# One token loop for q and k, DRAM-source transposes, and a do-projection moved into the attention loop: a linear-attention and MQA gradient kernel on one core

## The chip, the cores and the metric

The kernel runs on one core of one Trainium2 chip. The metric is the time of one execution on the device in microseconds (us); lower is better.

Terms: PE is TensorE and PEld its weight load, DVE is VectorE, ACT is ScalarE, POOL is GpSimd, SP is SyncE. "SPq" and "ACTq" are these engines' sequencers at work on issuing DMAs. The profile names a DMA transpose DMA_TRANSPOSE and an ordinary copy DMA_DIRECT2D; the trace holds a record of every packet that the DMA engines moved, with its size and duration.

## The reference, cut to what matters

Two attention blocks stand side by side, their outputs are concatenated, and all gradients are wanted (nine outputs in all). A is linear attention (16 heads of 28), B is softmax attention with one shared key and value head. S is 2048 tokens, D is 448, everything is bf16.

```python
def _A_ref(x, wqkv, wo):
    qkv = (x @ wqkv).reshape(B, S, 3, H, Dh) ...          # q, k, v
    phi = lambda t: jnp.where(t > 0, t + 1, jnp.exp(t)) + 1e-6
    pq, pk = phi(q), phi(k)
    kv = jnp.einsum("bhsd,bhse->bhde", pk, v);  z = jnp.einsum("bhsd->bhd", pk)
    o = einsum(pq, kv) / (einsum(pq, z)[..., None] + 1e-6)
    return o.reshape(B, S, D) @ wo
def _B_ref(x, wq, wk, wv, wo):
    # q has 16 heads, k and v one head; softmax(q k^T / sqrt(Dh)) v, then @ wo
...
_out, _vjp = jax.vjp(_f, ...);  _grads = _vjp(grad_out)    # grad_out is [1, 2048, 896]: A's half, B's half
```

448 = 3 x 128 + 64. The matmuls here contract over at most 128 partitions at a time (128*128 in the trace), so each operand with 448 rows is kept as three full chunks and one of 64 rows.

## The kernel before

Phase A computes A forward and backward; `phase_B_pre` prepares B; a loop of 540 units does B's attention forward and backward; a tail makes the last projections. Operands that must have the feature dimension on the partitions are transposed by DMA out of SBUF, from tiles that are padded to 512 columns:

```python
def dma_T(dst, src, t0, n):                      # SBUF -> SBUF, 4 token tiles a call
    nc.sync.dma_start_transpose(dst[:, t0:t0 + n, :, :].rearrange("p t c k -> p (t c) k"),
                                src[:, t0:t0 + n, :].rearrange("p t d -> p (t d)"))
...
load_nat(ga, go2[:, 0:D], nc.sync)               # grad_out, A's half
...
nc.gpsimd.memset(t[:, :, D:512], 0.0)            # for t in (pk, pq, wq_n, ga): the padding
...
for q4 in range(4):
    dma_T(gaT, ga, 4 * q4, 4)
```

q is projected after k's loop, in four groups, with GpSimd at work on every token tile:

```python
def phi(ps, dst, eng):
    E = awk.tile([P, D], F32, name="phiE")
    nc.scalar.activation(out=E[:], in_=ps[:, :], func=ACT.Exp)
    eng.tensor_scalar(out=E[:], in0=E[:], scalar1=1.0, scalar2=1e-6, op0=ALU.min, op1=ALU.add)   # POOL for q
    nc.vector.scalar_tensor_tensor(out=dst, in0=ps[:, :], scalar=0.0, in1=E[:], op0=ALU.max, op1=ALU.add)
...
def den(q4):                                     # divides by the denominators
    ...
        nc.gpsimd.tensor_tensor(out=wd, in0=wd, in1=rb, op=ALU.mult)
        nc.vector.tensor_tensor(out=pv, in0=pv, in1=rb, op=ALU.mult)
    dma_T(pqpT, pq, 4 * q4, 4)
```

Three names recur. `st1` is the first matmul of A's backward loop over tokens (`KOT` with `gaT`). `out1` is the loop that writes the gradient of A's x, from `pkT`, `gqT` and `gkT`. The do-projection (`do_nat`) multiplies B's half of grad_out by wo and stands at the end of `phase_B_pre`:

```python
for st in range(NS):                             # 16 token tiles
    ps = gen([P, 512])
    for c in range(4):
        mm(ps[:, :], gbT[:, st, c, :], woTp[:, c, :], start=(c == 0), stop=(c == 3))
    nc.any.tensor_copy(out=do_nat[:, st, :], in_=ps[:, :])
```

Of the kernel before, what the change touches and what calls it, by code (L numbers as in the profile page):

```python
# [14 lines left out]
H = 16  # L15
# [9 lines left out]
def kernel(  # L25
# [50 lines left out]
    make_identity(nc, identF[:])  # L76
# [26 lines left out]

    def chunks_of(i):
        lo, hi = HR[i]
        return [k for k in range(4) if k * P < hi and k * P + DC_ROWS[k] > lo]
# [4 lines left out]
    def phase_A(pa, cA, awk, psA):  # L111
# [15 lines left out]
        xaT, tT, gaT, pqpT = v4(R2), v4(tTf), v4(gaB), v4(ppB)  # L127
        gkn = wq_n

        qs = [nc.sync, nc.scalar]  # L130
        for i in range(8):
            if i == 2:
                load_w(w3, A_wqkv, D, 2 * D, nc.scalar)
            qs[i % 2].dma_start(xa[:, 2 * i:2 * i + 2, 0:D],
                                Ax2[i * 256:(i + 1) * 256, :].rearrange("(t p) d -> p t d", p=P))
# [5 lines left out]
        nc.gpsimd.memset(xa[:, :, D:512], 0.0)  # L141
        nc.gpsimd.memset(xa[:, :, D:D + 16], 1.0)
        nc.gpsimd.memset(w3[64:128, 3, :], 0.0)
        nc.gpsimd.memset(w3[0:64, 3, 3 * D:1408], 0.0)
        nc.gpsimd.memset(w3[:, 0:3, 3 * D:1408], 0.0)
        for t in (pk, pq, wq_n, ga):
            nc.gpsimd.memset(t[:, :, D:512], 0.0)
# [26 lines left out]
        K1T = [ppB[:, 4 * i:4 * i + 4, :] for i in range(2)]  # L174
# [7 lines left out]
        for t in (kv_blk, kvT_blk, dkv_blk, KO, KOT, zrow, *ddT):  # L182
            nc.gpsimd.memset(t[:], 0.0)
        for i in range(2):
            nc.gpsimd.memset(K1T[i], 0.0)

# [15 lines left out]
        def phi(ps, dst, eng):  # L202
            E = awk.tile([P, D], F32, name="phiE")
            nc.scalar.activation(out=E[:], in_=ps[:, :], func=ACT.Exp)  # L204
            eng.tensor_scalar(out=E[:], in0=E[:], scalar1=1.0, scalar2=1e-6, op0=ALU.min, op1=ALU.add)  # L205
            nc.vector.scalar_tensor_tensor(out=dst, in0=ps[:, :], scalar=0.0, in1=E[:], op0=ALU.max, op1=ALU.add)

# [10 lines left out]

        k1acc = accs()
        xT(0)  # L220
        xT(1)
        for st in range(NS):
            if st + 2 < NS:
                xT(st + 2)
            phi(proj(st, D), pk[:, st, 0:D], nc.vector)
            if st >= 2:
                accmm(k1acc, xa, pk, st - 2)
        accmm(k1acc, xa, pk, NS - 2)
        accmm(k1acc, xa, pk, NS - 1)
        nc.vector.tensor_tensor(out=zrow[64:80, :], in0=k1acc[3][64:80, :], in1=mrow[64:80, :], op=ALU.mult)  # L230
        hilo(K1T, k1acc)
        for i in range(2):
            nc.sync.dma_start_transpose(K1[i][:].rearrange("p c h k -> p (c h) k"), flat(K1T[i]))
        for q4 in range(4):
            dma_T(gaT, ga, 4 * q4, 4)
# [24 lines left out]
        def qproj(q4):  # L260
            for st in range(4 * q4, 4 * q4 + 4):
                phi(proj(st, 0), pq[:, st, 0:D], nc.gpsimd)
            dma_T(tT, pq, 4 * q4, 4)

        def den(q4):
# [8 lines left out]
            for s in range(4):  # L274
                st = 4 * q4 + s
                rb = rden[:, st, :].unsqueeze(2).to_broadcast([P, H, DH])
                wd = wq_n[:, st, 0:D].rearrange("p (h e) -> p h e", e=DH)
                pv = pq[:, st, 0:D].rearrange("p (h e) -> p h e", e=DH)
                nc.vector.tensor_scalar(out=wq_n[:, st, 0:D], in0=pq[:, st, 0:D], scalar1=-1e-6, scalar2=1.0,
                                        op0=ALU.add, op1=ALU.min)  # L280
                nc.gpsimd.tensor_tensor(out=wd, in0=wd, in1=rb, op=ALU.mult)
                nc.vector.tensor_tensor(out=pv, in0=pv, in1=rb, op=ALU.mult)
            dma_T(pqpT, pq, 4 * q4, 4)

        qproj(0)
# [3 lines left out]
        qproj(1)  # L289
        blkprod(kv_blk, [lambda c, i: K1T[0][:, c, i * P:(i + 1) * P], lambda c, i: K1T[1][:, c, i * P:(i + 1) * P]],  # L290
                [lambda c: w3[:, c, 2 * D:3 * D]])
        den(0)
        qproj(2)
        prod_to(KOT, woA, kvT_blk, True)
        prod_to(KO, kvT_blk, woA, False)
        den(1)
        qproj(3)
        den(2)

        wvT = w_T(cA.tile([P, 4, D], BF16, name="wvT"), w3, 2 * D)  # L300
        woT = w_T(cA.tile([P, 4, D], BF16, name="woT"), woA, 0)
# [5 lines left out]
        def st1(st):  # L307
            ps = gen([P, D])
            for c in range(4):
                mm(ps[:, :], gaT[:, st, c, :], KOT[:, c, :], start=(c == 0), stop=(c == 3))  # L310
            tps[st] = ps
            pr = awk.tile([P, H, DH], F32, name="phiE")
# [4 lines left out]
        def st2(st):  # L317
            pt = gen([P, P], BF16)
            nc.tensor.transpose(pt[:, :], ga[:, st, 3 * P:512], identB[:, :], tile_position=(0, 0))
            nc.vector.tensor_copy(out=ddT[st % 3][64:80, :], in_=pt[64:80, :])  # L320
# [7 lines left out]
        def outA(st):  # L328
# [5 lines left out]
            nc.sync.dma_start(out0[st * P:(st + 1) * P, 0:D], ot[:])  # L334

        for i in range(NS + 2):
            if i == 2:
                den(3)
# [26 lines left out]
        def gw(gn, blk):  # L365
# [3 lines left out]
            for c in range(4):  # L369
                r = DC_ROWS[c]  # L370
                sb = awk.tile([P, 512], BF16, name="osb")[:, 0:D]
                nc.any.tensor_copy(out=sb[0:r, :], in_=al[c][0:r, :])
                nc.sync.dma_start(out_2[c * P:c * P + r, blk * D:(blk + 1) * D], sb[0:r, :])
# [4 lines left out]
        for st in range(NS):  # L378
# [3 lines left out]
            dph = awk.tile([P, 512], BF16, name="osb")[:, 0:D]  # L382
            nc.gpsimd.tensor_scalar(out=dph[:], in0=pk[:, st, 0:D], scalar1=-1e-6, scalar2=1.0, op0=ALU.add, op1=ALU.min)  # L383
            nc.vector.tensor_tensor(out=gkn[:, st, 0:D], in0=ps[:, :], in1=dph[:], op=ALU.mult)
        xb = pk
        nc.gpsimd.memset(xb[:, :, D:512], 0.0)
        load_nat(xb, Bx2, nc.sync)
        prod_to(VWT, dkvT_blk, wvT, False)
        blkprod(dkv_blk, [lambda c, i: GT[0][:, c, cs(i)], lambda c, i: GT[1][:, c, cs(i)]], [lambda c: woT[:, c, :]])
        gkT = gaT  # L390
# [24 lines left out]
        wst = dkv_blk  # L415
        load_w(wst, B_wq, 0, D, nc.sync)
        wkv = awk.tile([P, 2, 4, DH], BF16, name="wkvst", bufs=1)
        load_w(wkv[:, 0, :, :], B_wk, 0, DH, nc.sync)
        load_w(wkv[:, 1, :, :], B_wv, 0, DH, nc.sync)
        wq_pad = K1[0].rearrange("p c h k -> p c (h k)")  # L420
        rep = K1[1].rearrange("p c h k -> p (c h k)")[:, 0:1024].rearrange("p (w c k) -> p w c k", w=2, k=P)
        wo_pr = ga[:, 0:4, :]
        woTp = v4(ga[:, 4:8, :]).rearrange("p c h k -> p c (h k)")
        nc.gpsimd.memset(wq_pad, 0.0)
        nc.gpsimd.memset(rep, 0.0)
        nc.gpsimd.memset(wo_pr, 0.0)
# [4 lines left out]
        for w in range(2):  # L431
            for j in range(4):
                nc.gpsimd.tensor_copy(out=rep[:, w, 0:3, 32 * j + 1:32 * j + 1 + DH], in_=wkv[:, w, 0:3, :])
                nc.gpsimd.tensor_copy(out=rep[0:64, w, 3, 32 * j + 1:32 * j + 1 + DH], in_=wkv[0:64, w, 3, :])
        for h in range(H):
            g, j = divmod(h, 4)
            nc.sync.dma_start(wo_pr[32 * j + 1:32 * j + 1 + DH, g, 0:D], B_wo[h * DH:(h + 1) * DH, :])

        gw(gkn, 1)
        xbT = v4(wq_n)  # L440
        for q4 in range(4):
            dma_T(xbT, xb, 4 * q4, 4)
        for g in range(4):
            nc.sync.dma_start_transpose(woTp[:, :, g * P:(g + 1) * P], wo_pr[:, g, :])
        nc.sync.dma_start(wo_d[:, :].rearrange("(g p) c -> p g c", p=P), wo_pr)
        gb = xa
        load_nat(gb, go2[:, D:2 * D], nc.sync)
# [3 lines left out]
        for st in range(NS):  # L451
# [7 lines left out]
            nc.any.tensor_copy(out=ot[:], in_=ps[:, :])  # L459
            nc.sync.dma_start(out1[st * P:(st + 1) * P, :], ot[:])  # L460

        gbT = gaT
        for q4 in range(4):
            dma_T(gbT, gb, 4 * q4, 4)
        return xb, xbT, gbT, wq_pad, rep, woTp, pq

    def phase_B_pre(pa, cA, awk, psA, io):
        xb, xbT, gbT, wq_pad, rep, woTp, pqr = io
        kT, vT, vaug, kn, qT, do_nat = kT_rep, vT_rep, vaug_, kn_, R1, R2
# [3 lines left out]

        for qc in range(NQC):
            for w, dst in [(0, kT), (1, vT)]:
                ps = gen([P, 512])
                for c in range(4):
                    mm(ps[:, :], rep[:, w, c, :], xbT[:, 4 * qc:4 * qc + 4, c, :], start=(c == 0), stop=(c == 3))
                nc.any.tensor_copy(out=dst[:, qc * 512:(qc + 1) * 512], in_=ps[:, :])  # L479
        ones16 = cA.tile([P, H], BF16, name="ones16")  # L480
        nc.gpsimd.memset(ones16[:], 1.0)
        bsel = pqr[:, 4, :].rearrange("p (g k) -> p g k", k=P)
        nc.gpsimd.memset(bsel, 0.0)
        for g in range(4):
            for j in range(4):
                nc.gpsimd.memset(bsel[32 * j:32 * j + 32, g, 4 * g + j:4 * g + j + 1], 1.0)
        kmx = cA.tile([H, NQC], F32, name="kmx")
        for qc in range(NQC):
# [8 lines left out]
        for j in range(4):  # L497
            nc.gpsimd.memset(kT[32 * j:32 * j + 1, :], -1.0)
            nc.gpsimd.memset(vT[32 * j:32 * j + 1, :], -1.0)
        shift = flat(pqr[:, 0:4, :])[0:H, 0:S]  # L500
        for qc in range(NQC):
            pn = gen([P, 512])
            for g in range(4):
                ps = gen([P, 512])
                for c in range(4):
                    mm(ps[:, :], wq_pad[:, c, g * P:(g + 1) * P], xbT[:, 4 * qc:4 * qc + 4, c, :], start=(c == 0),
                       stop=(c == 3))
                qs_ = qT[:, g, qc * 512:(qc + 1) * 512]
                nc.scalar.activation(out=qs_, in_=ps[:, :], func=ACT.Copy)
                sq = awk.tile([P, 512], BF16, name="osb")  # L510
                nc.vector.tensor_tensor(out=sq[:, :], in0=qs_, in1=qs_, op=ALU.mult)
# [353 lines left out]
```

## Time and profile before

| | |
|---|---|
| median of 3 runs | 1261.11 us (1260.49 to 1261.15) |
| first Exp of B's attention loop | 338.7 us |
| from there to the end (loop and tail) | 920.9 us |
| PE busy in the loop's steady part (20 us stretches) | 19.3 to 19.5 of 20 us |
| ACT busy in the same | 19.4 to 19.7 of 20 us |

The page shows the span in 40 equal slices of 31.5 us; each digit is the busy share of a slice in tenths, and DMA is the mean share of the 16 DMA engines. These are some of its lines for the kernel before.

```profile
PE   6768969699499999999999999999999999999878
...
POOL 8473073022047787878777877778787778778300
...
DMA  9436836934399999999999999999999998997783
...
DMA packets 690914, 204.96 MB, mean 163 GB/s; under 512 B 652464, under 2 KB 686640, under 8 KB 690736
```

From the twelfth slice to the fourth from the end runs the attention loop, where PE has a 9 in every slice; the last three are the tail. Only the first eleven digits, some 340 us, can gain much from this change, and there PE is far from full. What holds it up is in the chain of waits, the work that ended last followed back from the end. Its columns are the start in us, the length in us, and what it was.

```profile
46.29 1.70 POOL phiE L205
48.07 1.70 POOL phiE L205
...
64.56 5.21 POOL wdq L281 x4
...
96.55 4.87 DVE pq L282 x4
...
164.83 1.70 POOL osb L383
...
189.80 1.71 POOL osb L383
...
323.09 2.21 SPq L538
325.34 2.88 SPq L538
```

From 46 to 105 us the chain goes over phi of q on GpSimd (1.70 us a tile) and over the division; from 165 to 191 us it is one GpSimd pass of sixteen such tiles (`osb L383`), and at 323 us it is SP issuing small transposes (`L538`) while everything waits for the loop to start. The change attacks just these places.

### The profile page before, as it was taken

What the parts mean: (1) busy time and instruction counts of PE and PEld (TensorE: products, weight loads), DVE (VectorE), ACT (ScalarE), POOL (GpSimd) and SP (SyncE); (2) the same over time, 40 slices, a digit from 0 to 9 for tenths busy, and PEclk for the clock granted to TensorE, in tenths of its full rate; (3) what the DMA queues carried; (4) which work ended last, traced back from release to release, by engine and by line L of the source; (5) the groups of instructions that cost most, each with busy time, mean ns of one, the idle gap of its engine ahead of it and who ended that gap; (6) DMA issues with size and microseconds to landing.
All of it is one profiled execution on the core that took longest, in us unless ns stands there. A gap on an engine that the chain in (4) does not pass through costs nothing.

```text
span 1259.6 us, 38409 instructions
## 1 busy us (share of the span) xinstructions
PE 1136.0 (90%) x15382; PEld 457.1 (36%) x15388; DVE 876.8 (70%) x1601; ACT 904.9 (72%) x1788; POOL 781.1 (62%) x861
## 2 busy tenths in 40 slices
PE   6768969699499999999999999999999999999878
PEld 3433425344133333333333333333333333333334
DVE  5559621012059998989898989998999989899402
ACT  3321201135499999999999999999999999997212
POOL 8473073022047787878777877778787778778300
PEclk9879988799669999999999999999999999999889
DMA  9436836934399999999999999999999998997783
GB/s 239 78 67 118 159 99 138 221 87 68 110 194 183 166 174 189 183 172 181 180 166 183 190 163 187 186 182 170 187 186 172 183 184 160 196 187 127 218 166 110
DMA packets 690914, 204.96 MB, mean 163 GB/s; under 512 B 652464, under 2 KB 686640, under 8 KB 690736
## 3 DMA queue, kind: packets, MB, share of 16 engines
q1 hardware_dynamic: 684880, 198.51, 90.1%
q10 hardware_dynamic: 5856, 4.01, 1.0%
q8 instruction: 120, 1.97, 0.6%
q14 instruction: 58, 0.48, 0.1%
HBM read 24.93 MB, written 15.03 MB: 32 GB/s over the span
## 4 chain that ended last, share of the span: by engine, by line
PE 56%; ACT 20%; issue 8%; POOL 5%; DVE 4%; SPq 4%; DMA 2%; ACTq 0%; POOLq 0%; DVEq 0%
PE dk_acc L576 15%; PE oq L576 10%; PE agen L79 10%; ACT eT L634 9%; ACT cp L631 9%; PE sps L576 7%; PE dps L576 5%; PE dv_acc L576 2%; PE aacc L79 2%; POOL osb L383 2%; PE pgen L79 2%; POOL phiE L205 2%; PE sps L690 1%; SPq L87 1%; PE pacc L79 1%
## 5 line engine op out<-in xcount | busy, mean ns | idle before, releaser
L632 POOL TENSOR_TENSOR dsT<-cp,eT 128x512 bf16<-128x512 bf16 x512 | 590.7, 1154 | 176.7 <-ACT cp L631 138.3
L629 DVE TENSOR_TENSOR dsT<-dps,eT 128x512 bf16<-128x512 f32 x512 | 348.6, 681 | 59.5 <-PE dps L576 36.0
L745 DVE STREAM_TRANSPOSE dsx<-dsT 128x512 f32<-128x512 f32 x512 | 358.1, 700 | 1.0
L576 PEld LDWEIGHTS <-R_65 32*128 32x128 bf16 (+1 forms) x8192 | 174.3, 93 | 420.8 <-issue 375.7
L624 ACT ACTIVATE eT<-sps 128x512 bf16<-128x512 f32 x512 | 307.5, 601 | 20.0 <-PE dps L576 15.5
L631 ACT ACTIVATE cp<-dps 128x512 bf16<-128x512 f32 x512 | 305.4, 596 | 10.2 <-PE dps L576 10.1
L634 ACT ACTIVATE eT<-sps 128x512 bf16<-128x512 f32 x512 | 311.9, 609 | 0.0
L576 PE MATMUL dk_acc<-dsx,qX 32*32 32x512 bf16 x4096 | 289.5, 377 | 0.0
L576 PE MATMUL sps<-R_63,R_65 32*128 32x256 bf16 x2048 | 254.0, 281 | 19.9 <-ACT eT L624 16.2
L576 PE MATMUL dps<-doT,R_65 32*128 32x256 bf16 x2048 | 261.2, 273 | 7.0 <-DVE dsT L629 0.3
L576 PE MATMUL oq<-eT,R_65 128*32 128x256 bf16 x2048 | 218.1, 283 | 0.5
L576 PE MATMUL oq<-dsT,R_65 128*32 128x256 bf16 x2048 | 203.7, 279 | 0.3 <-ACT R_63 L739 0.2
L576 PEld LDWEIGHTS <-qX 32*32 32x32 bf16 x4096 | 69.9, 89 | 93.1 <-issue 52.0
L576 PE MATMUL dv_acc<-eN,don 128*32 128x512 bf16 x1024 | 86.1, 385 | 0.0
L736 DVE COPY oTs<-oq 64x256 f32<-64x256 f32 x64 | 26.7, 417 | 59.3 <-ACT eT L624 39.8
L662 POOL TENSOR_TENSOR don<-R_64,rl 128x128 bf16<-128x128 bf16 x64 | 25.8, 403 | 42.5 <-DMA eN<-eT 42.5
L204 ACT ACTIVATE phiE<-agen 128x448 f32<-128x448 f32 x32 | 17.3, 543 | 42.2 <-PE agen L79 31.1
L333 ACT ACTIVATE osb<-agen 128x448 bf16<-128x448 f32 x16 | 8.7, 543 | 44.4 <-PE agen L79 42.3
L205 POOL TENSOR_SCALAR phiE<-phiE 128x448 f32<-128x448 f32 x16 | 27.3, 1706 | 20.5 <-DVE zrow L230 15.7
L490 DVE TENSOR_TENSOR osb<-R_65 32x512 bf16<-32x512 bf16 x4 | 1.6, 411 | 53.6 <-ACT R_65 L479 53.6
L79 PE MATMUL agen<-R_65,R_64 128*128 128x448 bf16 x128 | 33.2, 405 | 6.2 <-ACT R_64 L192 4.5
L576 PEld LDWEIGHTS <-don 128*32 128x32 bf16 x1024 | 34.8, 98 | 0.5
(197 smaller groups left out, 1023.0 us busy)
## 6 DMA issues: line engine op xcount, KB each, us to landing
qX<-qn_d SPq DMA_DIRECT2D x128, 64.0 KB
out_dram<-osb SPq DMA_DIRECT2D x60, 112.0 KB
eN<-eT SPq DMA_TRANSPOSE x256
qn_d<-pk SPq DMA_DIRECT2D x1, 2048.0 KB
on_d<-onat SPq DMA_DIRECT2D x8, 256.0 KB
onat_B<-on_d SPq DMA_DIRECT2D x1, 2048.0 KB
ga<-in_grad_out_dram SPq DMA_DIRECT2D x4, 448.0 KB
pk<-in_B_x_dram SPq DMA_DIRECT2D x4, 448.0 KB
```

Source lines behind the costliest of these rows:

```text
L79: nc.tensor.matmul(out_ap, lhsT=lhsT, rhs=rhs, start=start, stop=stop, tile_position=(0, 0))
L205: eng.tensor_scalar(out=E[:], in0=E[:], scalar1=1.0, scalar2=1e-6, op0=ALU.min, op1=ALU.add)
L383: nc.gpsimd.tensor_scalar(out=dph[:], in0=pk[:, st, 0:D], scalar1=-1e-6, scalar2=1.0, op0=ALU.add, op1=ALU.min)
L576: nc.tensor.matmul(out, lhsT=lhsT, rhs=rhs, start=start, stop=stop, tile_position=pos, skip_group_check=True)
L624: nc.scalar.activation(out=et[:, u % 2, 0, :], in_=sp[0][:, :], func=ACT.Exp, scale=scale)
L629: nc.vector.tensor_tensor(out=dst[:, 0, :], in0=dp[0][:, :], in1=ew[:, w % 2, 0, :], op=ALU.mult)
L631: nc.scalar.activation(out=cp[:, :], in_=dp[1][:, :], func=ACT.Copy)
L632: nc.gpsimd.tensor_tensor(out=dst[:, 1, :], in0=cp[:, :], in1=ew[:, w % 2, 1, :], op=ALU.mult)
L634: nc.scalar.activation(out=et[:, u % 2, 1, :], in_=sp[1][:, :], func=ACT.Exp, scale=scale)
L662: nc.gpsimd.tensor_tensor(out=dn[:], in0=dnv, in1=r_[:].to_broadcast([P, 2, 2, 32]), op=ALU.mult)
L736: nc.vector.tensor_copy(out=oTs[v // 8][:, :], in_=oq[0:64, 0:256])
L745: nc.vector.transpose(out=dsx[b][:, tp, :, :, :].rearrange("p h t c -> p (h t c)").bitcast(F32), in_=dsT[y][:, :, :].rearrange("p h c -> p ...
```

## The change

Its intent is to take GpSimd out of the work on tokens, to run q's projection in k's token loop, to read transposed operands straight from DRAM without a padded copy in SBUF, and to move the do-projection into the first units of the attention loop, where PE has no gradient work yet. The diff, cut to its core (cuts are marked):

```diff
+    def dram_T(dst, x2d, c0):
+        for c in range(4):
+            r = DC_ROWS[c]                                  # 128, 128, 128, 64
+            nc.sync.dma_start_transpose(dst[0:r, c, :], x2d[:, c0 + c * P:c0 + c * P + r])
...
+        nc.gpsimd.memset(gaT[64:128, 3, :], 0.0)
+        dram_T(gaT, go2, 0)
-        for q4 in range(4):
-            dma_T(gaT, ga, 4 * q4, 4)
...
-    def phi(ps, dst, eng):
-            E = awk.tile([P, D], F32, name="phiE")
-            eng.tensor_scalar(out=E[:], ...)
+    def phi(ps, dst, E):                                    # E and tm are bf16
+            nc.vector.tensor_scalar(out=tm[:], in0=E, scalar1=1.0, scalar2=1e-6, op0=ALU.min, op1=ALU.add)
...
         for st in range(NS):
             ...
-            phi(proj(st, D), pk[:, st, 0:D], nc.vector)
+            kproj(st)
             if st >= 2:
                 accmm(k1acc, xa, pk, st - 2)
+            if st >= LAG:                                   # LAG = 5
+                qproj(st - LAG)
...                                                          # den: reciprocals spread by ACT, two bf16 products on DVE
+                nc.vector.tensor_tensor(out=pq[:, st, 0:D], in0=pq[:, st, 0:D], in1=rx, op=ALU.mult)
+                nc.vector.tensor_tensor(out=wq_n[:, st, 0:D], in0=wq_n[:, st, 0:D], in1=rx, op=ALU.mult)
...
-        load_nat(xb, Bx2, nc.sync)                          # and four dma_T later
+        dram_T(xbT, Bx2, 0)
...
+    def do_T():                                             # called in the out1 loop
+        nc.gpsimd.memset(gbT[64:128, :, 3, :], 0.0)
+        for st in range(NS):
+            rows = slice(st * P, (st + 1) * P)
+            nc.sync.dma_start_transpose(gbT[:, st, 0:3, :], go2[rows, D:D + 3 * P])
+            nc.sync.dma_start_transpose(gbT[0:64, st, 3:4, :], go2[rows, D + 3 * P:2 * D])
...                                                          # in the attention loop, unit u, v = u - 1:
+                if v < NS and v >= 0:
+                    ps = psD.tile([P, 512], F32, name="dps")
+                    for c in range(4):
+                        mm(ps[:, :], gbT[:, v, c, :], woTp[:, c, :], start=(c == 0), stop=(c == 3))
+                    nc.vector.tensor_copy(out=do_nat[:, v, :], in_=ps[:, :])
```

## The prediction

> **What bounds it now.** Busy time by stretch shows three parts. The attention loop of B (337 to about 1170 us) has PE and ACT busy 97%; the change barely touches it, nor the tail (90 us). Before 337 us the chain of waits runs through GpSimd: phi of q on POOL (16 x 1.71 us) and the two `rden` products (POOL 1.28, DVE 1.21 us each) fill 45 to 105 us; the POOL `dph` pass fills 165 to 191 us (16 x 1.70). From 229 to 246 us and from 321 to 337 us the chain is SP issuing DMA transposes.
>
> **What the change removes.** The q phase merges into the k loop (DVE about 0.6 us a pass), denominators become bf16 multiplies, `dph` goes to DVE. I estimate 30 us saved by about 100 us and 12 us at `dph`. The do-projection (16 x 4 matmuls of 0.4 us, 20 to 25 us with evictions) leaves the stage before B and costs about 8 us in the first 16 units, where no D part runs. With waits for DMA (20 us): 60 to 75 us in sum.
>
> **What it adds.** 448 columns are 3 x 128 + 64, and in the compiled order the 64-column part of each DRAM transpose is not a DMA transpose but a plain copy of single elements: `gaT` (64x2048x1), `xbT` (64x2048x1) and 16 of 64x128x1 for `gbT`. The Trainium skill ("DMA: Bandwidth & Descriptors", DMA Transpose, Constraints, and Rules for kernel authors) says that a DRAM input with a free dim under 128 can fall back to a rearranged pattern, and that a non-contiguous last dim costs one descriptor per element. Then each set is 131,072 packets of 2 bytes, 393,216 in all. The DMA records of this trace show 896-byte packets at about 44 ns, 256 at 18, 56 at 10, 4 at 9: about 8 ns at zero size. Over 16 engines: 66 us a set at best; I take 90 (11 ns). The skill's "19x slower" (VectorE: DVE Perf Modes, The three transpose paths) on a 128-column transpose (2048 packets x 18 ns / 16 = 2.3 us) would give only 22 us; no record here is that short.
>
> **On the critical path.** All sit in the SP queue. `gaT`'s piece stands ahead of the tT and K1 transposes that den needs: it ends near 115 us, so the st1 loop starts near 130 instead of 96. `xbT`'s piece and five `gbT` pieces stand ahead of most gkT transposes, which out1 needs: out1 runs near 340 instead of 229. Eleven `gbT` pieces (62 us) stand ahead of the qn transposes and shift rows: the loop starts near 440 to 455 instead of 337. Each ns per packet moves the total by about 25 us.
>
> **Prediction: 1390 us, 8 in 10 between 1275 and 1640.** Faster by over 2%: 0.11; within 2%: 0.09; slower: 0.80.
>
> **What would show it.** Packets of 2 bytes, about 393,000 with DMA busy at low GB/s; PE nearly idle from about 65 to 120 and from 230 to 330 us; loop start past 400 us; POOL nearly idle before the loop; den and out1 waiting for DMA.
>
> **What would make it wrong.** Packets near 3 ns: the pieces hide, and the total falls to 1190. Packets of 20 ns or more from scattered 2-byte reads: over 1600. The queue not holding back what stands behind the element copies.

## More of the kernel before

For the start of the loop, this is the group of its first Exp, with the first and last start in us:

```profile
L624 ACT ACTIVATE eT<-sps x512: 597/597/608, 338.7 to 1150.2; 128x512 bf16<-128x512 f32 x171
```

## The result, and the profile after

The changed kernel is correct and takes 1672.42 us in the median of 4 runs (1671.74 to 1673.81), against 1260.8 us for the kernel before in the same rounds. The ratio is 1.3269 (95% interval 1.3246 to 1.3292). Ratios here are the mean time of one kernel's runs over that of the other's of the same rounds, so they are not quite the ratio of the medians quoted.

The same lines of the page, after the change (a slice is now 41.8 us):

```profile
PE   7400099400004107749999999999999999999969
...
POOL 5000000200000000004778777777777787778800
...
DMA  9999987999999999258999999999999999999593
GB/s 166 2 2 2 63 154 145 56 27 2 2 2 54 33 29 44 53 129 152 169 169 184 172 187 185 167 186 176 186 179 174 191 167 189 173 169 196 92 266 101
DMA packets 1074371, 200.52 MB, mean 120 GB/s; under 512 B 1039952, under 2 KB 1070096, under 8 KB 1074192
```

GpSimd has indeed gone from the work on tokens. But PE now has zeros in slices 3 to 5, 9 to 12 and 15, and in slices 3, 4 and 10 to 12 the DMA engines are full while they move 2 GB/s. There are 383,457 packets more than before and fewer bytes. The DMA records of the trace hold 393,216 packets of 2 bytes, where the kernel before has none: 3 x 131,072, which is 64 columns x 2048 tokens for each of three operands.

The chain of waits, by engine, has moved from PE and GpSimd to SP's issuing (before: POOL 5%, SPq 4%):

```profile
PE 40%; SPq 33%; ACT 15%; issue 6%; DMA 3%; POOL 1%; DVE 1%; ACTq 0%; DVEq 0%; POOLq 0%
```

SP's own timeline shows where (start in us, length in us, line, operation, operands):

```profile
23.18 0.72 SPq L107 DMA_DIRECT2D gaT<-in_grad_out_dram  x1
24.02 170.35 SPq L100 DMA_TRANSPOSE wvT<-R_65  x4
...
341.56 0.65 SPq L107 DMA_DIRECT2D pk<-in_B_x_dram  x1
342.30 163.61 SPq L90 DMA_TRANSPOSE gaT<-wdq  x1
...
545.28 10.08 SPq L489 DMA_TRANSPOSE R_64<-in_grad_out_dram  x1
555.46 0.53 SPq L443 DMA_DIRECT2D out_dram<-osb  x1
556.03 0.62 SPq L490 DMA_DIRECT2D R_64<-in_grad_out_dram  x1
556.69 9.38 SPq L489 DMA_TRANSPOSE R_64<-in_grad_out_dram  x1
```

Lines 107 and 490 are the calls that transpose 64 columns. The profile names them DMA_DIRECT2D, an ordinary copy, where the calls for 128 columns are DMA_TRANSPOSE. Issuing the copy takes SP 0.7 us; the next DMA in its queue then needs long to be issued at all: 164 us for the single transpose behind `xbT`'s copy, 166 of the 170 us for the first of the four behind `gaT`'s, and about 10 behind a piece of `gbT`. While SP stands still, PE does too. These stretches of 20 us have, after stretch and length, the busy time of PE, PEld, DVE, ACT and POOL, then PE's granted clock, the DMA share and GB/s (a DMA share of 1.95 means that nearly two packets overlap on every engine, on average):

```profile
100.00:120.00 20.00, 0.00 (x0) 0.00 (x0) 0.00 (x0) 0.00 (x0) 0.00 (x0) 0.50 1.95 2
...
440.00:460.00 20.00, 0.00 (x0) 0.00 (x0) 0.00 (x0) 0.00 (x0) 0.00 (x0) 0.50 1.95 2
```

And the loop starts late:

```profile
L652 ACT ACTIVATE eT<-sps x512: 597/597/609, 733.5 to 1561.2; 128x512 bf16<-128x512 f32 x171
```

733.5 instead of 338.7 us is 394.8 us of the loss; from there to the end it is 938.4 instead of 920.9 us, another 17.5.

How long is one packet? In 80 to 180 us nothing else runs, so the DMA view of that stretch gives the rate directly:

```profile
DMA packets 79769, 0.16 MB, mean 2 GB/s; under 512 B 79769, under 2 KB 79769, under 8 KB 79769
...
q1 hardware_dynamic: 79769, 0.16, 194.9%
```

100 us x 16 engines / 79,769 packets is 20.1 ns per packet and engine. A whole set took 166.8 us (`gaT`) and 161.6 us (`xbT`). The third set runs in sixteen pieces of 8,192 packets; a piece that stands alone took about 7.5 us, 14.6 ns per packet and engine.

### The profile page after: what moved, and what is told of

Read it like the earlier page. It is cut to its first block, busy times and chain, and to the rows that moved or that the text cites. A ratio compares the mean times of both kernels' runs of the same rounds, so it can differ in the third digit from the quotient of the medians.

```text
span 1671.9 us, 38450 instructions
## 1 busy us (share of the span) xinstructions
PE 1127.2 (67%) x15388; PEld 453.4 (27%) x15388; DVE 876.4 (52%) x1657; ACT 906.2 (54%) x1800; POOL 691.6 (41%) x815
## 4 chain that ended last, share of the span: by engine, by line
PE 40%; SPq 33%; ACT 15%; issue 6%; DMA 3%; POOL 1%; DVE 1%; ACTq 0%; DVEq 0%; POOLq 0%
PE dk_acc L598 12%; SPq L90 11%; SPq L100 11%; PE oq L598 7%; ACT eT L662 7%; ACT cp L659 6%; PE agen L78 6%; PE sps L598 5%; SPq L489 5%; PE dps L598 4%; PE dv_acc L598 2%; PE aacc L78 1%; PE sps L718 1%; DMA out_dram<-osb 1%; PE dps L78 1%
## 5 line engine op out<-in xcount | busy, mean ns | idle before, releaser
L652 ACT ACTIVATE eT<-sps 128x512 bf16<-128x512 f32 x512 | 307.7, 601 | 35.7 <-PE dps L598 17.5
L598 PE MATMUL sps<-R_63,R_65 32*128 32x256 bf16 x2048 | 250.6, 278 | 32.4 <-ACT eT L652 28.0
L78 PE MATMUL agen<-ga,kv 128*128 128x512 bf16 (+1 forms) x20 | 6.0, 438 | 192.5 <-ACT osb L442 192.5
L291 ACT CAST KOT<-agen 128x448 bf16<-128x448 f32 (+1 forms) x7 | 3.7, 531 | 159.0 <-PE agen L78 158.8
```

The costliest lines, as they stand in the source:

```text
L78: nc.tensor.matmul(out_ap, lhsT=lhsT, rhs=rhs, start=start, stop=stop, tile_position=(0, 0))
L598: nc.tensor.matmul(out, lhsT=lhsT, rhs=rhs, start=start, stop=stop, tile_position=pos, skip_group_check=True)
L652: nc.scalar.activation(out=et[:, u % 2, 0, :], in_=sp[0][:, :], func=ACT.Exp, scale=scale)
```

## The experiments

The theory: the single-element packets account for the whole loss. Rivals: other parts of the change are slow themselves; or the packets would hide if they stood elsewhere. A further question is why a packet took 20 ns when larger ones had led the prediction to 11.

### e1: all three sets as DMA transposes

```diff
+    xs_d = dpool.tile([S, P], BF16)                 # DRAM scratch; the same for gs_d
+        for h_ in range(2):                          # the 64 columns twice, so that 128 are there
+            nc.scalar.dma_start(xs_d[:, 64*h_:64*h_+64], Bx2[:, 3*P:D])
+            nc.scalar.dma_start(gs_d[:, 64*h_:64*h_+64], go2[:, D+3*P:2*D])
-        dram_T(gaT, go2, 0)
+        dram_T(gaT, go2, 0, go2[:, 3*P:4*P])         # 128 columns; the last 64 belong to B
-        dram_T(xbT, Bx2, 0)
+        dram_T(xbT, Bx2, 0, xs_d[:, :])
-            nc.sync.dma_start_transpose(gbT[0:64, st, 3:4, :], go2[rows, D+3*P:2*D])
+            nc.sync.dma_start_transpose(gbT[:, st, 3:4, :], gs_d[rows, :])
```

The surplus 64 rows are finite and meet zero rows of the weights, so they add nothing; the memsets of `gaT`, `xbT` and `gbT` go away with them.

> All three sets of single-element copies are replaced by DMA transposes of a 128-column piece (the 64 columns are copied twice, side by side, into a DRAM scratch with 128-byte packets; for gaT the 64 neighbouring columns of grad_out serve). Theory (the 393,216 packets of 2 bytes, at 20 ns a packet and engine, cost everything): the waits of the changed kernel at 60-209 us (144 us to give back), 342-520 us (about 185) and the stretched out1 loop (about 110) go away, so about 1672 - 439 = 1233 us, between 1205 and 1250, with no packet of 2 bytes. Rival (the rest of the change is itself slower, for instance the transposes read from DRAM and the do-projection in the first units): above 1265 us.

Measured: 1249.74 us (4 runs), correct; ratio to before 0.9925 (0.9902 to 0.9949). No packet of 2 bytes is left, and 422.7 us came back out of a loss of 411.6. The theory holds for the loss, and the rival falls: the rest of the change is not slower than the kernel before. But it landed at the upper end of the range, and at less than 1% gain the rest of the change is worth far less than the 60 to 75 us of the prediction. That became the second question (e5, e6, e9).

### e2, e3, e4: one set of single elements at a time

Each is e1 with one set put back as in the changed kernel: `gaT` (e2), `xbT` (e3), the sixteen pieces of `gbT` (e4).

```diff
-        dram_T(gaT, go2, 0, go2[:, 3*P:4*P])         # e2
+        nc.gpsimd.memset(gaT[64:128, 3, :], 0.0)
+        dram_T(gaT, go2, 0)
```

> As e1, but gaT's 64 columns are copied by single elements again. Theory: e1 plus about 144 us, some 1375 us; 131,072 packets of 2 bytes over about 165 us, and the transposes behind them in the SP queue issued only then. Rival (the packets hide behind other work, as they could at 90 us a set): e1 plus under 60 us.

> As e1, but xbT's 64 columns are copied by single elements. Theory: e1 plus about 160 us (162 us of packets, hardly any PE work to hide them), some 1390 us. Rival as in e2.

> As e1, but the sixteen 64x128 pieces of gbT are copied by single elements. Theory: e1 plus 90 to 140 us, some 1345 us, because the first pieces stand ahead of gkT and the last ahead of the qn transposes, and part of them hides behind PE work. If the three excesses add up to the 439 us of e1, the sets cost independently; if they add to much less, they share waits.

Measured (one run each): 1393.92, 1405.01 and 1367.49 us, which is 144.2, 155.3 and 117.8 us over e1. All three lie close to what was expected over e1. They add up to 417.2, against 422.7 for all three together. The three sets cost independently. (e3 and e4 also drop two of e1's four copies into the scratch, whose price is the subject of e5, so their shares come out a few us too small.) Little hides: `gaT`'s packets ran from 28.6 to 194.9 us, 166 us, and all but 22 of these reached the total.

### e5: the price of the repair

In e1, ScalarE issued the four copies into the scratch before its first Exp. They move to GpSimd's queue, behind its memsets.

```diff
-            nc.scalar.dma_start(xs_d[...], ...)      # two for xs_d, two for gs_d
+            nc.gpsimd.dma_start(xs_d[...], ...)      # after the last memset of the start
```

> e1, with the four copies into the scratch issued by GpSimd after its memsets instead of by ScalarE ahead of its first Exp. In e1 ScalarE issued them from 11.8 to 22.3 us, and the token loop started at 24 us instead of 13. Theory (those 10 us were the price of the repair, not of the change): about 1240 us, 8 to 11 us less than e1's 1249.7. Rival (the token loop is not on the critical path there): no difference.

Measured: 1240.16 us (4 runs), ratio 0.9843 (0.9822 to 0.9864). 9.6 us less than e1, as expected: these were the repair's cost, not the change's.

### e6: the do-projection back before the loop

```diff
-                if v < NS and v >= 0: ...            # out of the loop's units 1 to 16
+        woTp = pqr[:, 0:4, :]                        # end of phase_B_pre, four DMA transposes of wo_d
+        for st in range(NS):
+            ps = gen([P, 512])
+            for c in range(4):
+                mm(ps[:, :], gbT[:, st, c, :], woTp[:, c, :], start=(c == 0), stop=(c == 3))
+            nc.any.tensor_copy(out=R2[:, st, :], in_=ps[:, :])
```

> e5, with the do-projection back in the stage before the loop, at its end, where PE idles from about 270 to 306 us while SP issues transposes. Theory (the move cost time: 16 x 1.0 us of matmuls and a wait for woTp came into the loop's first units, and left a gap in which they had been free): 12 to 20 us less than e5, about 1224 us. Rival (the prediction's: the stage before B gets longer by about 20 us and the loop shorter by 8): about 12 us more than e5.

Measured: 1224.12 us (4 runs), ratio 0.9721 (0.9704 to 0.9737), 16.0 us less than e5. The first Exp of the loop, in e5:

```profile
L658 ACT ACTIVATE eT<-sps x512: 597/597/608, 301.1 to 1126.5; 128x512 bf16<-128x512 f32 x171
```

And in e6:

```profile
L662 ACT ACTIVATE eT<-sps x512: 597/597/609, 301.2 to 1113.8; 128x512 bf16<-128x512 f32 x171
```

The loop starts at the same time with and without the do-projection ahead of it, because its first Exp waits for a DMA that SP issues late: the stores of `wkvT_d`, at 292 to 296 us in both. The wait lists of 268 to 303 us (engine and line, what it waited for, us in total, times, longest) show it, in e5 and in e6:

```profile
ACT L658 <- DMA wkvT_d<-osb: 29.1, 1, 29.1
...
ACT L662 <- DMA wkvT_d<-osb: 13.6, 1, 13.6
```

PE's busy time by stretch shows the gap that was there, in e5:

```profile
280.00:300.00 20.00, 0.00 (x0) 0.00 (x0) 0.00 (x0) 0.19 (x1) 0.00 (x0) 0.50 0.38 120
```

So in e5 the move bought nothing at the start, and from the first Exp to the end e5 took 934.1 us where e6 took 920.6, like the kernel before (920.9). Moving the do-projection cost 13.5 us there, and not the 8 of the prediction. (These are the profiled runs; e5's was its fastest of four, 1237.11 us, which is why the medians differ by 16.0.)

### e7: two queues

e2 with half of the tokens issued by ScalarE, and the small loads of B's weights moved to SP so that ScalarE has no DMA right behind.

```diff
-        dram_T(gaT, go2, 0)
+        for c in range(3): ...                       # the full chunks as they were
+        nc.sync.dma_start_transpose(gaT[0:64, 3, 0:S//2], go2[0:S//2, 3*P:D])
+        nc.scalar.dma_start_transpose(gaT[0:64, 3, S//2:S], go2[S//2:S, 3*P:D])
```

> e2 (gaT's 64 columns by single elements), with half of the tokens issued from SP and half from ScalarE. Theory G (SP's own generation of descriptors sets the rate of 0.8 packets a ns, 20 ns per packet and engine): two issuers run at twice the rate, the packets are over in about 85 us, each record shorter than 39 ns, and the total is 60 to 80 us under e2's 1393.9. Theory M (the 16 engines or the memories behind them set the rate): still about 165 us, total within 15 us of e2.

Measured (one run): 1403.57 us. The packets, half in each queue, took 172.5 us, 21.1 ns per packet and engine. Theory M holds. The Trainium skill says it in "DMA: Bandwidth & Descriptors", Issuing engines are not separate DMA queues: DMAs from several engines run on the same 16 DMA engines. This trace agrees: 172.5 us with two queues, 166.2 with one (e2).

### e8: a packed source

```diff
+        nc.sync.dma_start(ga_d[:, :], go2[:, 3*P:D])               # 2048 x 64, packed
-        nc.sync.dma_start_transpose(gaT[0:64, 3, :], go2[:, 3*P:D])
+        nc.sync.dma_start_transpose(gaT[0:64, 3, :], ga_d[:, :])
```

> e2, with the 64 columns first copied to a packed DRAM tensor of 2048x64, so that the element copy reads 2 bytes every 128 bytes instead of every 1792. If scattered reads of DRAM set the 20 ns, the packets get faster (under 130 us for the set, total under 1370). If the cost is per packet wherever it reads, still about 165 us, total 1394 to 1400.

Measured (one run): 1400.09 us, the packets 168.2 us. How far apart the reads lie in DRAM does not matter here.

### e9: two more steps out of SP's queue

```diff
-    def do_T(): ...                                  # 32 DRAM transposes, and the scratch gs_d
+        load_nat(xa, go2[:, D:2*D], nc.sync)         # after the last use of xa
+        for q4 in range(4):
+            dma_T(gbT, xa, 4*q4, 4)                  # out of SBUF, as in the kernel before
...                                                   # and the 8 transposes and 2 stores for wkvT_d, from the
                                                      # end of phase_B_pre to before out1
```

> e6 with two more steps taken out of the SP queue: gbT's 32 DRAM transposes (1.2 us of issue each, standing ahead of xbT and gkT while PE idles from 145 to 175 us) become 4 loads and 4 transposes out of SBUF, as in the kernel before; and the 8 small transposes for wkvT, needed by the tail only, are issued before out1 instead of behind the qn transposes (10 us of issue at 290-300 us with PE idle). Theory (SP's issue time is now the limit of these stretches): 1224 minus about 15 minus about 10, near 1200 us. Rival (PE or the loop's start limit): within 5 us of e6.

Measured: 1210.84 us (4 runs), correct; ratio to before 0.9592 (0.9576 to 0.9608). 13.3 us less than e6, where about 25 were expected; the theory has the direction, and half the size. The loop starts at:

```profile
L653 ACT ACTIVATE eT<-sps x512: 597/597/609, 287.9 to 1100.6; 128x512 bf16<-128x512 f32 x171
```

The matmuls of `gw(gkn)` (the gradient of A's k weights; `gw(gqn)`, below, is that of its q weights) start at 166.1 us instead of 181.1 in e6, so the first step gave its 15 us there. By the end of B's q projections (264.5 instead of 267.6 us) only 3 were left: out1 waits in its turn. Between there and the loop's start, where the second step acts, another 10 came. This version beats both kernels.

### e10: the element copy in ScalarE's queue

```diff
-        nc.sync.dma_start_transpose(gaT[0:64, 3, :], go2[:, 3*P:D])
+        nc.scalar.dma_start_transpose(gaT[0:64, 3, :], go2[:, 3*P:D])    # B's weights loaded by SP instead
```

> e2, with gaT's element copy issued from ScalarE's queue, so that no transposes stand behind it in SP's. Theory (blocking by queue order, on top of the duration): tT, K1 and den get through beside the packets, st1 starts as soon as gaT has landed at about 200 us, some 20 us earlier than in e2: about 1374 us. Rival (the packets fill all 16 engines, so everything stands still whichever queue they are in): within 8 us of e2's 1393.9.

Measured (one run): 1410.11 us, outside both expectations. The experiment did not separate the theories, because it ran into a third thing. SP's wait list (engine and line, what it waited for, us in total, times, longest):

```profile
SPq L102 <- DMA gaT<-in_grad_out_dram: 173.8, 1, 173.8
```

The four `wvT` transposes in SP's queue did go through beside the packets of ScalarE's queue: their 256-byte packets stand in the records between 30 and 39 us, at 116 ns on average up to 36 us instead of 21 before the copy began, and SP issued each of the four in 1.2 to 1.3 us. So the element copy held up issuing behind it in its own queue (e2), and not issuing from the other (e10). Then SP waited for `gaT` by name. The program rotates its DMAs, from whichever queue, over eight completion semaphores (100 and 102 to 108 in the trace), and a DMA waits until the last user of its semaphore has landed; the element copy has semaphore 100, and so has the first `woT` transpose, the next in the rotation. So in this program one very long DMA also holds up the queue whose turn it is when the rotation comes back to its semaphore. In the changed kernel the profile shows SP's issue itself taking some 165 us, and no such wait. What the queue order alone costs stays open; the gain looked for here was 20 us of 411.

### e11 to e14: what sets 20 ns

All four are e2 with other packets for `gaT`'s last chunk. In e11, e13 and e14 the data are wrong on purpose; the comparison with the reference passed all the same, so that chunk's share of the outputs is below its tolerance, and "correct" does not vouch for this chunk in the other runs.

```diff
# e11: 65,536 packets of 4 bytes
+        nc.sync.dma_start(gaT[0:64, 3, :].bitcast(F32).unsqueeze(2),
+                          go2.bitcast(F32)[0:1024, 160:224].rearrange("t d -> d t").unsqueeze(2))
# e12: 131,072 packets of 2 bytes into DRAM, then 64 rows into SBUF
+        nc.sync.dma_start(ga_d[:, :].unsqueeze(2), go2[:, 3*P:D].rearrange("t d -> d t").unsqueeze(2))
+        nc.sync.dma_start(gaT[0:64, 3, :], ga_d[:, :])
# e13 (so, do = 320, 1) and e14 (321, 0): 65,472 packets of 4 bytes, one side off by 2 bytes
+        nc.sync.dma_start(gaT[0:64, 3, do:do+2046].rearrange("p (t k) -> p t k", k=2),
+                          go2[0:1023, so:so+128].rearrange("t (d k) -> d t k", k=2))
```

> e2, with 65,536 packets of 4 bytes instead of 131,072 of 2 (same bytes, same 64 partitions; the data in gaT's last chunk are wrong on purpose, so the gradients of A come out wrong). Cost per packet: half the time, about 83 us, total near 1394 - 83 = 1311. Cost per byte: still 165 us, total 1394.

> e2, with the elements written to a DRAM tensor of 64 rows, and the rows then loaded into gaT. If writing 2 bytes into SBUF is what slows the packets from 7 to 20 ns after their first 4,000, they get faster here (set under 120 us, total under 1360). If the reads of 2 bytes or the engines themselves are, still about 165 us or more, total 1395 or more.

Measured (one run each): e11 1268.09 us, e12 2513.95 us. e11 missed both of its figures. e12 missed its theory; the letter of its other branch ("165 us or more") holds, but nobody had forecast eight times that. e11's packets were not only half as many, each was also faster. The DMA view of e11, 32 to 60 us:

```profile
q1 hardware_dynamic: 47596, 0.19, 184.1%
```

28 us x 16 / 47,596 is 9.4 ns per packet and engine, so the cost is neither per packet nor per byte: 4 bytes cost less than half of what 2 do. And e12 showed that the destination matters, in the wrong direction for its theory: the 131,072 packets into DRAM took 1275 us, 156 ns each. That left the write of part of a word as the suspect, and e13 and e14 were made for it.

> e11, with 65,472 packets of 4 bytes whose destination in SBUF starts 2 bytes off a 4-byte word (sources aligned; data of gaT's last chunk wrong on purpose). e11's packets ran at 9.4 ns per packet and engine in their steady part, the 2-byte ones at 20.0. Theory W (a write that covers a 4-byte word only in part is what doubles the time): 20 ns or more, set over 75 us, total about 1300. Theory N (only the packet's size or the reading matters): 9.4 ns, total as e11's 1268.

> As e13, but the destination is aligned and the source in DRAM starts 2 bytes off a 4-byte word. Theory W: 9.4 ns, total about 1268. If partial reads are what costs: 20 ns, total about 1300.

Measured (one run each): e13 1319.12 us, e14 1266.82 us. The DMA view of e13, 32 to 60 us:

```profile
q1 hardware_dynamic: 20854, 0.08, 191.8%
```

And of e14, the same stretch:

```profile
q1 hardware_dynamic: 47431, 0.19, 184.4%
```

With the destination 2 bytes off, a 4-byte packet takes 28 x 16 / 20,854 = 21.5 ns; with the source 2 bytes off it takes 9.4 ns, as in e11. Theory W holds against theory N: what doubles the time is writing into SBUF so that a 4-byte word is covered only in part. In e2 and in e13 the neighbouring packet covers the rest of the same word, so these runs do not tell a partial write as such from two packets that share a word. How the DMA engine comes to the double time is not shown either.

## Why the prediction was wrong, point by point

- **The mechanism was right.** The 64-column pieces became copies of single elements, 393,216 packets of 2 bytes, as the prediction read from the compiled order and from the Trainium skill ("DMA: Bandwidth & Descriptors", DMA Transpose, Constraints, and Rules for kernel authors); PE idled in the stages that it named, only for longer (60 to 209 us where it had said 65 to 120), the loop started after 400 us, and GpSimd was nearly idle before it. Forecast slower with 0.80, and it was. Yet 1672.42 us lies outside 1275 to 1640.
- **The step that failed is "66 us a set at best; I take 90 (11 ns)".** A set took 166.8 and 161.6 us, 20 ns a packet. The prediction drew a line through the lengths of records of 896, 256, 56 and 4 bytes and read it at 2. e11 to e14 show why that line does not reach 2: a packet that covers a word in SBUF only in part costs twice what a 4-byte packet into a whole word does. Even at 4 bytes the line was right by luck: e11's records last 17.3 ns each (28 us x 16 x 1.841 / 47,596), nearly two at a time on an engine, and only so come to 9.4 ns a packet. The first 3,500 or so packets of a set run at about 6 to 7 ns before the rate settles at 20 (from 25.5 to 26.5 us in the changed kernel's records 2,456 packets start, 6.5 ns each), so a look at a short burst would have misled as well. The prediction had named the case, "Packets of 20 ns or more from scattered 2-byte reads: over 1600", but the reads were not the reason: packing them (e8) or moving them off by 2 bytes (e14) changed nothing. By the prediction's own rule, "each ns per packet moves the total by about 25 us", the 9 ns missing are worth 225 to 235 us: about 1620. Measured directly, the three sets cost 422.7 us (e1), where the prediction's sums leave 189 to 204 for them (1390 - 1261 + 60 to 75).
- **The second mis-sized term is "60 to 75 us in sum".** With the packets gone and the repair's own cost taken out (e5), the rest of the change is worth 1259.3 - 1240.2 = 19 us. Before the loop it gains 338.7 - 301.1 = 37.6 us. st1's loop starts at 69.0 instead of 91.4 us (22 us, 30 expected). The 12 us of the `dph` pass did not show up: `gw(gkn)` starts 26.9 us earlier (180.5 instead of 207.4) where the last matmul of `gw(gqn)` before it starts 28.5 us earlier (131.5 instead of 160.0). There SP issues `gbT`'s 32 transposes ahead of `xbT` and `gkT`, and taking these out (e9) moved that point by 15 us. The do-projection was expected to free 20 to 25 us before the loop, and freed none (e5 and e6 start the loop at 301.1 and 301.2 us); in the loop it took 13.5 us (8 expected, e6). These 40 to 55 us too much of expected gain close the rest: about 1620 plus 50 is 1670.
- **"The skill's 19x"** (VectorE: DVE Perf Modes, The three transpose paths: a plain copy with a strided access pattern for the transpose is 19 times slower than the crossbar when the innermost stride of the destination is large) was rightly not relied on. Here it is the source that is read in large steps (1792 bytes), and the elements of a destination row are neighbours. A set moves half the data of a 128-column transpose, which is an estimated 2.3 us of packets, and takes 166.8 us: 70 times for half the data, or about 145 for the same.
- **"All sit in the SP queue"** describes what happened. Whether another queue would have helped was tried (e10) and not settled.

## What to carry to other kernels

Look at what a transpose call has become, not at its name: in this profile a transpose call that shows as DMA_DIRECT2D, with packets of 2 bytes, is an element copy, and DMA full at 2 GB/s with every engine at zero was its mark. A feature dimension of 448, not a multiple of 128, was cheaper here to round up (borrow neighbouring columns, or copy the rest into a padded scratch, and let zero weights cancel it) than to transpose exactly: 1249.74 us (e1) against 1672.42. Moving work "to where PE is free" pays only if its old place was on the critical path: here it filled a gap in which PE waited for SP to issue DMAs.

## What the Trainium skill lacked or had wrong

- "DMA: Bandwidth & Descriptors", Rules for kernel authors, says that a strided last dim gives one descriptor per element but gives no price for an element of 2 bytes. Here it was 20 ns per 2-byte element and engine into SBUF (e2: 131,072 in 166.2 us) and 156 ns into DRAM (e12: 1275 us).
- The same page, Specifications, says that transfers under 512 B are read-modify-write. No run here tests 512 B, but they show a step that this does not cover, since all of these packets are far smaller: 4-byte packets into whole words of SBUF took 9.4 ns (e11), the same packets 2 bytes off took 21.5 ns (e13), and a source 2 bytes off cost nothing (e14: 9.4 ns). No page has this.
- "VectorE: DVE Perf Modes", The three transpose paths, gives 19x for a strided copy against the crossbar, for a large innermost stride of the destination. It has no figure for this case, 2-byte elements read from DRAM in steps of 1792 bytes into neighbouring places of SBUF; these runs show about 145x for the same data (166.8 us for half the data of an estimated 2.3 us transpose).
- "DMA: Bandwidth & Descriptors" does not say that an engine's issue stands still behind a DMA of very many packets in its own queue. Here SP needed some 165 us to issue the transpose behind 131,072 of them, but 1.2 to 1.3 us with the copy in ScalarE's queue (e10); and where the program rotates its DMAs over eight semaphores, one such DMA held up the other queue for 173.8 us (e10).
